# Moving V's base copy from VectorE to GpSimd through an fp32 staging tile, with one more VectorE exponential batch and a longer ride allowance

## The chip, the cores and the metric

One core of a Trainium2 chip is used; the jobs ran on two chips, 0 and 6, and every kernel is compared with the kernel before in its own job. The metric is device time in microseconds (us) of one execution; a kernel is run three to twelve times and the median is quoted. Engines: PE is TensorE (matmul), PEld its weight loads, DVE is VectorE, ACT is ScalarE, POOL is GpSimd.

## The reference

Multi-head attention for x of 2048 x 448, 16 heads of 28:

```python
qkv = (x @ wqkv).reshape(B, S, 3, H, Dh).transpose(2, 0, 3, 1, 4)
q, k, v = qkv[0], qkv[1], qkv[2]
scores = einsum("bhqd,bhkd->bhqk", q, k) * Dh ** -0.5
o = einsum("bhqk,bhkd->bhqd", softmax(scores), v)
out = o.transpose(0, 2, 1, 3).reshape(B, S, D) @ wo
```

## The kernel before

The work is cut into 16 units: one group of four heads times 512 queries. A unit has 16 key tiles times 4 heads = 64 score tiles of 128x512 in PSUM. Most of them go through ACT (exponential, to bf16 slots in `PT`), in groups of three and two tiles. The others, four key tiles of each unit, five in the units of `D_FIVE` and three in the last, are "batches" for DVE: an integer approximation of the exponential, made as a sum of four terms. A batch costs DVE four evictions (`PD` from PSUM, one for each head) and two int16 steps, and it costs PE four PV passes instead of one. All PV passes of a unit accumulate in one PSUM bank (`ACC`), which DVE copies out (`OTS`) when the unit is complete; I say that a unit closes then. Units are numbered from 0 to 15.

```python
D_FIVE = (3, 5, 7, 9, 11)
...
NPT = 36                                  # PT slots for exponentials
VX = sb("VX", [128, 3, 2 * GD], FP32)     # GD = 112
...
P.pool("M", [5, 6])                       # two PSUM banks for projections and DVE score tiles
```

V of a group and a chunk of 512 keys is projected into a bank of `M`; DVE reads that bank twice, once for the bf16 base copy `V` and once for the key tiles that batches need, as fp32 `VX`, from which POOL makes four scaled copies `VC`:

```python
def proj_v(g, c, prio):
    ... # 16 matmuls into one bank
    ev1, ev2 = job(f"pv_{g}_{c}", prio, mms,
                   (Vd <- bank[:, 0:4*GD]),                       # base copy, bf16
                   extra=(tensor_copy VX[:, xs, 0:nb*GD] <- some key tiles of bank))
    v_ev[(g, c)] = ev1
    for j in range(NTERM):                                         # NTERM = 4
        sc = P.add("pool", tensor_scalar VC <- VX * TERM_C[j], deps=[ev2, ...], dur=450)
```

(The lambdas are shortened here.) The order of instructions on each engine is not written by hand. The kernel has a list scheduler that simulates the engines with estimated durations when the kernel is built, and emits the order that it found. Part of it is the ride rule. Score matmuls of different heads use different rows of the PE array, so several issued together cost hardly more than one: in the trace of run C below, four issued together at 240.54 us took 0.40 us, a single one at 242.24 us 0.39 us. A score tile for DVE therefore waits for an ACT group with other heads to ride with, up to an allowance:

```python
RIDE = 8000.0     # ns
...
if op.ride:
    near = prev is not None and prev.kind == "r" and not self.burst & set(op.heads) and ...
    if not near:
        st = max(st, ready_t[i] + op.ride)
```

A last step puts filler matmuls of zeros into the gaps in PE's order that the scheduler foresees, to keep PE's activity up.

## Time and profile before

| kernel before | |
|---|---|
| median of the first three runs | 373.45 us (372.86 to 374.69) |
| busy PE, DVE, ACT | 93%, 92%, 93% of the span |
| busy POOL | 19% |

The profiled run is another one. It took 375.33 us (span 373.5 us), more than any of the timed runs, and its spans and idle times should be read with that in mind.

The page of the profile, cut to the lines that matter. Part 1 gives busy us, share of the span and the number of instructions by engine; part 4 the engines' shares of the chain of waits; part 5 the groups: line, engine, operation, output<-input, count | busy us, mean ns | idle us of the engine just before them and what ended it.

```profile
PE 346.7 (93%) x3953; PEld 108.7 (29%) x3953; DVE 342.2 (92%) x530; ACT 347.8 (93%) x306; POOL 70.9 (19%) x142
...
DVE 49%; PE 30%; ACT 14%; DMA 2%; issue 2%; SPq 0%
...
L898 ACT ACTIVATE PT<-ps 128x1024 bf16<-128x1024 f32 (+1 forms) x301 | 344.6, 1266 | 7.3 <-PE ps L857 5.5
L917 DVE TENSOR_SCALAR PD<-ps 128x512 int16<-128x512 f32 x272 | 177.4, 680 | 9.3 <-PE ps L857 7.6
L857 PE MATMUL ps<-QT,KT 28*128 28x512 bf16 x1024 | 149.0, 384 | 7.9 <-ACT PT L898 3.0
...
L925 DVE TENSOR_SCALAR PD<-PD 128x4096 int16<-128x4096 int16 x68 | 83.9, 1236 | 0.1
...
L712 POOL TENSOR_TENSOR QT<-RB,OTS 128x128 bf16<-128x128 f32 x60 | 36.1, 632 | 159.6 <-DMA RB<-scr_r 159.6
...
L923 DVE TENSOR_SCALAR PD<-PD 128x2048 int16<-128x2048 int16 x68 | 47.3, 703 | 0.1
...
L800 PE MATMUL ps<-ZM,ZW 128*32 128x512 bf16 x160 | 13.8, 383 | 0.0
```

Three engines are within one per cent of each other, and the chain of waits passes through all three. L857 are the score matmuls. L809 are the PV passes and L800 the fillers.

The groups of DVE with their shapes kept apart, the three lines of V's evictions:

```profile
L497 DVE CAST V<-ps 128x448 bf16<-128x448 f32 x16 | 9.8, 615 | 0.0
...
L551 DVE COPY VX<-ps 128x112 f32<-128x112 f32 x12 | 3.2, 264 | 0.0
L551 DVE COPY VX<-ps 128x224 f32<-128x224 f32 x4 | 1.5, 376 | 0.0
```

The second eviction is 4.7 us busy in all; by start times in the timeline it holds up the next instruction by 0.18 or 0.30 us each, 3.4 us in all.

Busy us of each engine in stretches (from:to, length, then PE, PEld, DVE, ACT, POOL, each with its count, then granted clock, DMA share, GB/s):

```profile
30.00:328.00 298.00, 283.60 (x3247) 86.35 (x3243) 294.03 (x447) 292.93 (x257) 54.58 (x101) 1.00 0.06 17
...
328.00:358.00 30.00, 27.99 (x307) 7.93 (x304) 27.15 (x43) 29.98 (x28) 4.39 (x8) 1.00 0.13 39
```

Up to 328 us DVE and ACT are both busy over 98% of the time; after that ACT alone is.

### The profile page before, as it was taken

The numbers are of one execution on the slowest core, as the hardware profiler recorded it, in microseconds if no ns is written. First come the engines' busy times: TensorE is split into PE (matmuls) and PEld (weight loads), VectorE is DVE, ScalarE is ACT, GpSimd is POOL, SyncE is SP. The second block draws the span as 40 slices with busy tenths as digits, with TensorE's granted clock in tenths as the row PEclk, the third lists the DMA queues.
The fourth block names the chain that finished last, engine by engine and source line by source line (L and its number), as shares of the span: only waits on it lengthen the run. The fifth ranks groups of instructions, "written<-read, shape, count | busy, mean of one in ns | idle before, by whom it ended". The sixth has DMA issues, their size and how long they took to land.

```text
span 373.5 us, 9127 instructions
## 1 busy us (share of the span) xinstructions
PE 346.7 (93%) x3953; PEld 108.7 (29%) x3953; DVE 342.2 (92%) x530; ACT 347.8 (93%) x306; POOL 70.9 (19%) x142
## 2 busy tenths in 40 slices
PE   7899999989999999998999999999998999999992
PEld 2342232323322323232223223332222223222231
DVE  1699999999999999999999999999999999999832
ACT  2799999999999999999999999999999999999971
POOL 7212021221401321041201303212030302002100
PEclk9899999999999999999999999999999999999998
DMA  9900010100001010010100000000000002110201
GB/s 172 194 21 2 12 37 2 32 2 18 16 3 32 3 31 2 4 31 2 32 2 14 21 5 29 2 10 24 21 12 4 31 15 67 38 29 18 80 0 58
DMA packets 21623, 10.49 MB, mean 28 GB/s; under 512 B 15757, under 2 KB 19597, under 8 KB 21577
## 3 DMA queue, kind: packets, MB, share of 16 engines
q1 hardware_dynamic: 20152, 9.54, 10.7%
q8 instruction: 32, 0.52, 0.6%
q10 hardware_dynamic: 1424, 0.31, 0.5%
q14 instruction: 15, 0.11, 0.1%
HBM read 5.66 MB, written 2.08 MB: 21 GB/s over the span
## 4 chain that ended last, share of the span: by engine, by line
DVE 49%; PE 30%; ACT 14%; DMA 2%; issue 2%; SPq 0%
DVE PD L917 24%; ACT PT L898 14%; PE ps L857 12%; DVE PD L925 11%; PE ps L809 10%; DVE PD L923 6%; PE ps L520 4%; DVE QT L495 2%; DVE OTS L695 2%; PE ps L542 2%; DMA xT<-in_x_dram 1%; DVE V L497 1%; DVE OUTS L679 1%; DVE KT L497 1%; PE ps L667 1%
## 5 line engine op out<-in xcount | busy, mean ns | idle before, releaser
L898 ACT ACTIVATE PT<-ps 128x1024 bf16<-128x1024 f32 (+1 forms) x301 | 344.6, 1266 | 7.3 <-PE ps L857 5.5
L917 DVE TENSOR_SCALAR PD<-ps 128x512 int16<-128x512 f32 x272 | 177.4, 680 | 9.3 <-PE ps L857 7.6
L857 PE MATMUL ps<-QT,KT 28*128 28x512 bf16 x1024 | 149.0, 384 | 7.9 <-ACT PT L898 3.0
L809 PE MATMUL ps<-PD,VC 128*32 128x512 bf16 x1088 | 91.3, 384 | 3.7 <-DVE PD L925 2.0
L925 DVE TENSOR_SCALAR PD<-PD 128x4096 int16<-128x4096 int16 x68 | 83.9, 1236 | 0.1
L857 PEld LDWEIGHTS ps<-QT,KT 28*128 28x128 bf16 x1024 | 38.2, 91 | 130.5 <-ACT PT L898 74.4
L809 PE MATMUL ps<-PT,V 128*32 128x512 bf16 x752 | 66.5, 384 | 3.5 <-DVE OTS L695 3.5
L712 POOL TENSOR_TENSOR QT<-RB,OTS 128x128 bf16<-128x128 f32 x60 | 36.1, 632 | 159.6 <-DMA RB<-scr_r 159.6
L558 POOL TENSOR_SCALAR VC<-VX 128x112 bf16<-128x112 f32 (+1 forms) x64 | 28.1, 438 | 121.9 <-DVE VX L551 118.9
L923 DVE TENSOR_SCALAR PD<-PD 128x2048 int16<-128x2048 int16 x68 | 47.3, 703 | 0.1
L520 PE MATMUL ps<-xT,w_raw 128*32 128x512 bf16 x512 | 39.8, 391 | 2.2 <-DVE PD L917 1.1
L809 PEld LDWEIGHTS ps<-PD,VC 128*32 128x32 bf16 x1088 | 22.7, 94 | 43.7 <-issue 15.9
L809 PEld LDWEIGHTS ps<-PT,V 128*32 128x32 bf16 x752 | 17.4, 94 | 32.3 <-issue 19.9
L542 PE MATMUL ps<-w_raw,xT 128*128 128x112 bf16 x256 | 19.1, 217 | 1.2 <-DVE PD L917 1.0
L542 PEld LDWEIGHTS ps<-w_raw,xT 128*128 128x128 bf16 x256 | 13.5, 99 | 11.5 <-issue 6.7
L520 PEld LDWEIGHTS ps<-xT,w_raw 128*32 128x32 bf16 x512 | 10.5, 95 | 21.5 <-issue 10.2
L800 PE MATMUL ps<-ZM,ZW 128*32 128x512 bf16 x160 | 13.8, 383 | 0.0
L667 PE MATMUL ps<-wop,QT 128*128 128x448 bf16 x48 | 13.2, 357 | 0.2 <-DVE PD L917 0.2
L497 DVE CAST KT<-ps 128x512 bf16<-128x512 f32 x16 | 11.0, 685 | 1.9 <-PE ps L520 1.8
L495 DVE TENSOR_SCALAR QT<-ps 128x512 bf16<-128x512 f32 x15 | 10.3, 686 | 0.2
L695 DVE COPY OTS<-ps 128x512 f32<-128x512 f32 x15 | 10.2, 679 | 0.1
L497 DVE CAST V<-ps 128x448 bf16<-128x448 f32 x16 | 9.8, 615 | 0.0
(49 smaller groups left out, 56.1 us busy)
## 6 DMA issues: line engine op xcount, KB each, us to landing
RB<-scr_r SPq DMA_DIRECT2D x60, 64.0 KB, 2.0
out_dram<-OUTS SPq DMA_DIRECT2D x16, 112.0 KB, 1.7
w_raw<-in_wqkv_dram SPq DMA_DIRECT2D x3, 249.0 KB, 4.1
wop<-in_wo_dram SPq DMA_DIRECT2D x16, 24.5 KB
w_raw<-in_wqkv_dram ACTq DMA_DIRECT2D x3, 87.0 KB, 4.2
scr_l<-OTS SPq DMA_DIRECT2D x15, 8.0 KB
LT<-scr_l SPq DMA_DIRECT2D x15, 8.0 KB, 1.7
scr_r<-RS SPq DMA_DIRECT2D x15, 8.0 KB, 1.4
```

The costliest lines, as they stand in the source:

```text
L495: fe = (lambda e: e.tensor_scalar(evac[0](), evac[1](hold[0].banks[0]), mul, None, ALU.mult))
L497: fe = (lambda e: e.tensor_copy(evac[0](), evac[1](hold[0].banks[0])))
L520: ins = e.matmul(ps[32 * h:32 * h + 32, b * 512:(b + 1) * 512], w_raw[:, it, col:col + 32], xT[:, it, c * 512:(c + 1) * 512], start=(it == ...
L542: ins = e.matmul(ps[:, b * 512 + j * GD:b * 512 + (j + 1) * GD], xT[:, it, n * 128:(n + 1) * 128], w_raw[:, it, 2 * D + g * GD:2 * D + (g ...
L558: sc = P.add("pool", (lambda e, dst=dst, j=j: e.tensor_scalar(dst, src, TERM_C[j], 1.0, ALU.mult, ALU.mult)), deps=[ev2, ms_c1[j]], after= ...
L712: nm = P.add("pool", (lambda e, k=k: e.tensor_tensor(QT[:, g, c * QCH + k * w_:c * QCH + (k + 1) * w_], RB[:, ub, k * w_:(k + 1) * w_], OT ...
L809: return e.matmul(ps[32 * h:32 * h + 32, ACC * 512:(ACC + 1) * 512], lhsT, rhs, start=first, stop=False, skip_group_check=True, tile_posit ...
L857: return e.matmul(bank(b), KT[32 * h:32 * h + DH, g, kt * 128:(kt + 1) * 128], QT[32 * h:32 * h + DH, g, c * QCH:(c + 1) * QCH], start=Tru ...
L898: ex = P.add("act", (lambda e, p0=p0, w=w, b0=b0: e.activation(PT[:, p0 * 512:(p0 + w) * 512], bank(b0, w), AF.Exp, scale=ESCALE)), deps=[ ...
L917: r = P.add("dve", (lambda e, hold=hold, zs=zs, h=h: e.tensor_scalar(PD[:, zs, 0, h * 512:(h + 1) * 512], bank(hold[0].banks[0]), ZBIAS, 0 ...
L923: h1 = P.add("dve", (lambda e, zs=zs: e.tensor_scalar(PD[:, zs, 1, :], PD[:, zs, 0, :], float(TERM_D[1]), None, ALU.add)), deps=rs_ + [z_l ...
L925: h2 = P.add("dve", (lambda e, zs=zs: e.tensor_scalar(PD[:, zs, 2:4, :], PD[:, zs, 0:2, :], float(TERM_D[2]), None, ALU.add)), deps=[h1] + ...
```

## The change

Its intent: let DVE read each V bank once, into an fp32 staging tile that holds all four key tiles; let POOL, which is idle most of the time, make the bf16 base copy from there; spend the DVE time that this frees on one more batch (in unit 13), which takes four score tiles off ACT. The ride allowance goes from 8 to 10 us.

```diff
-D_FIVE = (3, 5, 7, 9, 11)
+D_FIVE = (3, 5, 7, 9, 11, 13)
...
-        VX = sb("VX", [128, 3, 2 * GD], FP32)
+        VX = sb("VX", [128, 3, 4 * GD], FP32)
... (job() loses its second eviction)
-            ev1, ev2 = job(f"pv_{g}_{c}", prio, mms, ((lambda: Vd), ...), evac_dur=545,
-                           extra=((lambda e, b: e.tensor_copy(VX[:, xs, 0:nb * GD]..., bank(b)...[:, j0:4:js, :])), ...))
-            v_ev[(g, c)] = ev1
+            ev = job(f"pv_{g}_{c}", prio, mms,
+                     ((lambda: VX[:, xs, :]), (lambda b: bank(b)[:, 0:4 * GD]), vx_last[xs]), evac_dur=545)
+            v_ev[(g, c)] = []
+            for k in range(2):
+                Vd = V[:, 4 * c + 2 * k:4 * c + 2 * k + 2, ...]
+                vs = VX[:, xs, 2 * k * GD:(2 * k + 2) * GD]...
+                sc = P.add("pool", (lambda e, Vd=Vd, vs=vs: e.tensor_scalar(Vd, vs, 1.0, 1.0, ALU.mult, ALU.mult)),
+                           deps=[ev, ms_v1], after=[sc], dur=520, ...)
+                v_ev[(g, c)].append(sc)
... (the scaled copies now read VX with a step, and wait for ev)
-        RIDE = 8000.0
+        RIDE = 10000.0
```

More of the change, by code (lines that the diff above doesn't have):

```diff
@@ L479, in _fast, with job @@
         job_last = []
-        def job(name, prio, mm_ops, evac, evac_eng="dve", evac_dur=610, mul=None, extra=None):
+        def job(name, prio, mm_ops, evac, evac_eng="dve", evac_dur=610, mul=None):
             hold = []
@@ L497, in job @@
                 fe = (lambda e: e.tensor_copy(evac[0](), evac[1](hold[0].banks[0])))
-            if extra is None:
-                ev = P.add(evac_eng, fe, deps=[prev] + list(evac[2:]), dur=evac_dur, prio=-100.0, name=f"{name}_ev", rel=[(hold[0], 0)])
-                if prio > 0.5:
-                    job_last.append(ev)
-                return ev
-            ev1 = P.add(evac_eng, fe, deps=[prev] + list(evac[2:]), dur=evac_dur, prio=-100.0, name=f"{name}_ev")
-            ev2 = P.add("dve", (lambda e: extra[0](e, hold[0].banks[0])), deps=[prev] + list(extra[2:]), after=[ev1], dur=extra[1], prio=-100.0,
-                        name=f"{name}_ev2", rel=[(hold[0], 0)])
+            ev = P.add(evac_eng, fe, deps=[prev] + list(evac[2:]), dur=evac_dur, prio=-100.0, name=f"{name}_ev", rel=[(hold[0], 0)])
             if prio > 0.5:
-                job_last.append(ev2)
-            return ev1, ev2
+                job_last.append(ev)
+            return ev
         kq_ev = {}
@@ L547, in proj_v @@
             vx_n[0] += 1
-            Vd = V[:, 4 * c:4 * c + 4, g * 128:(g + 1) * 128].rearrange("p n (h r) -> p n h r", r=32)[:, :, :, 0:DH]
-            ev1, ev2 = job(f"pv_{g}_{c}", prio, mms,
-                           ((lambda: Vd), (lambda b: bank(b)[:, 0:4 * GD].rearrange("p (n h d) -> p n h d", n=4, d=DH)), ms_v1), evac_dur=545,
-                           extra=((lambda e, b: e.tensor_copy(VX[:, xs, 0:nb * GD].rearrange("p (n d) -> p n d", n=nb),
-                                                           bank(b)[:, 0:4 * GD].rearrange("p (n d) -> p n d", d=GD)[:, j0:4:js, :])), 130 + 90 * nb, vx_last[xs]))
-            v_ev[(g, c)] = ev1
-            src = VX[:, xs, 0:nb * GD].rearrange("p (n h d) -> p n h d", n=nb, d=DH)
-            sc = None
+            ev = job(f"pv_{g}_{c}", prio, mms,
+                     ((lambda: VX[:, xs, :]), (lambda b: bank(b)[:, 0:4 * GD]), vx_last[xs]), evac_dur=545)
+            sc = None
+            v_ev[(g, c)] = []
+            for k in range(2):
+                Vd = V[:, 4 * c + 2 * k:4 * c + 2 * k + 2, g * 128:(g + 1) * 128].rearrange("p n (h r) -> p n h r", r=32)[:, :, :, 0:DH]
+                vs = VX[:, xs, 2 * k * GD:(2 * k + 2) * GD].rearrange("p (n h d) -> p n h d", n=2, d=DH)
+                sc = P.add("pool", (lambda e, Vd=Vd, vs=vs: e.tensor_scalar(Vd, vs, 1.0, 1.0, ALU.mult, ALU.mult)),
+                           deps=[ev, ms_v1], after=[sc], dur=520, prio=g * 4 + c - 2.0, name=f"vb{g}_{c}_{k}")
+                v_ev[(g, c)].append(sc)
+            src = VX[:, xs, :].rearrange("p (n h d) -> p n h d", n=4, d=DH)[:, j0:4:js, :, :]
             for j in range(NTERM):
@@ L558, in proj_v @@
                 sc = P.add("pool", (lambda e, dst=dst, j=j: e.tensor_scalar(dst, src, TERM_C[j], 1.0, ALU.mult, ALU.mult)),
-                           deps=[ev2, ms_c1[j]], after=[sc], dur=450, prio=g * 4 + c, name=f"vc{g}_{c}_{j}")
+                           deps=[ev, ms_c1[j]], after=[sc], dur=450, prio=g * 4 + c, name=f"vc{g}_{c}_{j}")
             vc_ev[(g, c)] = sc
@@ L822, in pv_a @@
             op = pv_common(u, kt, f"PV{u}_{kt}", f_pv, list({id(tile_ev[(u, kt, h)]): tile_ev[(u, kt, h)] for h in range(4)}.values())
-                           + [v_ev[(g, kt // 4)]], u + (kt + 4) / NK)
+                           + v_ev[(g, kt // 4)], u + (kt + 4) / NK)
             for s in slots:
```

## The prediction

> **What bounds it now.** The page's busy line has PE 93%, DVE 92%, ACT 93%: three engines in balance. By stretches (the windows view), from 30 to 328 us DVE is busy 294.0 of 298 us and ACT 292.9; from 328 to 358 us ACT 29.98 of 30 and DVE 27.2. The chain of waits changes between DVE, PE and ACT until 331 us, then is one run of 24 exponentials to 358 us, then a serial end of 10 us. So DVE and ACT bind together to about 328 us, ACT alone after that.
>
> **Removed.** The second V eviction: 12 copies of 128x112 (264 ns) and 4 of 128x224 (376 ns). In the timeline they move the next start by only 0.18 and 0.30 us, so DVE wins 12*0.18+4*0.30 = 3.4 us. The first eviction now writes fp32 staging instead of bf16 V; I expect it to stay near 615 ns (the 128x512 evictions take 679 ns to fp32, 685 to bf16). Its PSUM bank comes free about 0.2 us sooner.
>
> **Added.** One VectorE batch: start to start 4*0.60+0.60+1.13 = 4.13 us of DVE, and three more PV passes on PE (0.22 us each, 0.65 us). ACT loses four of 752 tiles at 344.6/752 = 0.458 us: 1.83 us. GpSimd gets 32 casts of 128x224, about 0.43 us each as the scaled copies of that shape (1.71 us for four undisturbed), 14 us in all; it is busy only 71 us. It has to cast from SBUF, having no access to PSUM (Trainium skill, "GPSIMD Engine Reference", Specifications). Casts could queue behind the normalising multiplies that wait for a DMA, but V jobs run most of a unit ahead. At the start V of chunk 0 should be ready near 14.2 us; the first PV starts at 16.7.
>
> **Contention.** The Trainium skill ("SBUF — State Buffer", Who interferes with whom) says that a VectorE operation in a two-port mode and a GpSimd operation exclude each other. The trace agrees: scaled copies take 286 to 1422 ns, and the int16 DVE steps (medians 683, 1217 ns) reach 996 and 1527 when they meet GpSimd. I take today's DVE loss as about 3 us over 124 GpSimd operations, so 0.8 us more from 32 more (an estimate from these spreads).
>
> **On the path.** DVE: -3.4+4.1+0.8 = +1.5 us, but the new batch lies in unit 13, near 300-325 us, and the last two units have slack for most of it. ACT, which binds the end, gets 1.8 us shorter. PE +0.65 us, partly replacing filler matmuls. The larger ride allowance (8 to 10 us): about neutral. If ACT's own idle (7.3 us) doesn't grow, the kernel is 1.8 us shorter; I expect 0.3 us to be given back. The static order is computed anew; I allow 2 us either way for that.
>
> Predicted: 371.9 us, range 369.4 to 375.2; faster by over 2%: 3%, within 2%: 94%, slower: 3%.
>
> **What would show it.** Groups: exponentials near 342.8 us busy; PD evictions x276, int16 steps x69, their means up by 0-20 ns; staging copy 128x448 x16 near 615 ns; 32 POOL casts at 0.43-0.6 us. Busy line: DVE 342-345, POOL 86-90. No notable PE wait on POOL. Last exponential ending near 357 us.
>
> **What would make it wrong.** DVE the sole limit, so that +1.5 us shows in full and ACT's gain turns into idle (375); GpSimd locking out the int16 steps far oftener; V casts stuck behind a multiply that waits for its DMA; a slower fp32 eviction; or a reshuffled order that holds the two PSUM banks longer.

## The result, and the profile after

| | before | after |
|---|---|---|
| median of six runs, us | 373.5 (372.86 to 374.69) | 371.95 (371.26 to 372.73) |
| ratio | | 0.9954, 95% interval 0.9931 to 0.9977 |

A ratio is the mean time of one kernel's runs over that of the other's of the same rounds, so it is not quite the ratio of the medians quoted. Executions over 1.5% slower than the fastest of the same kernel are left out of the means. The change is within 2%, and it is a gain that the interval separates from zero.

The page after:

```profile
PE 342.3 (92%) x4033; PEld 110.3 (30%) x4033; DVE 342.8 (92%) x520; ACT 345.4 (93%) x304; POOL 83.7 (23%) x174
...
DVE 52%; PE 37%; ACT 5%; DMA 3%; issue 2%; SPq 0%; DVEq 0%
...
L894 ACT ACTIVATE PT<-ps 128x1536 bf16<-128x1536 f32 (+1 forms) x299 | 342.2, 1273 | 6.8 <-PE ps L853 5.1
L913 DVE TENSOR_SCALAR PD<-ps 128x512 int16<-128x512 f32 x276 | 180.4, 680 | 8.1 <-PE ps L853 7.0
L853 PE MATMUL ps<-QT,KT 28*128 28x512 bf16 x1024 | 140.1, 385 | 8.7 <-ACT PT L894 5.3
...
L921 DVE TENSOR_SCALAR PD<-PD 128x4096 int16<-128x4096 int16 x69 | 84.5, 1226 | 0.1
...
L919 DVE TENSOR_SCALAR PD<-PD 128x2048 int16<-128x2048 int16 x69 | 47.8, 698 | 0.1
...
L548 POOL TENSOR_SCALAR V<-VX 128x224 bf16<-128x224 f32 x32 | 15.7, 508 | 103.1 <-DVE VX L497 103.0
...
L796 PE MATMUL ps<-ZM,ZW 128*32 128x512 bf16 x228 | 18.9, 382 | 0.0
```

V's only eviction in the groups of DVE by shape, and the stretches:

```profile
L497 DVE COPY VX<-ps 128x448 f32<-128x448 f32 x16 | 9.8, 613 | 0.3 <-PE ps L535 0.2
```

```profile
30.00:328.00 298.00, 279.70 (x3349) 87.33 (x3345) 292.80 (x438) 293.84 (x257) 64.12 (x126) 1.00 0.06 17
328.00:358.00 30.00, 28.93 (x294) 8.79 (x294) 29.27 (x45) 29.62 (x26) 4.91 (x8) 1.00 0.15 43
```

What I had forecast of the parts is there: the eviction costs the same to fp32 (613 ns) as to bf16 (615 ns); DVE is busy 342.8 us (forecast 342 to 345) and ACT's exponentials 342.2 us (342.8); the 32 casts take 508 ns on average. The list of waits has one wait of a PE weight load on a cast, of 0.2 us. In the start, V of chunk 0 is cast from 13.3 to 14.0 us and the first PV begins at 16.6 us.

Two numbers were in no term of my sum. The score matmuls are busy 140.1 us instead of 149.0, although their count is the same; and the fillers grew from 160 to 228. The same number of score matmuls in less time means that they overlap more; run C below, where only the ride allowance differs, ties that to the allowance. Because of the fillers PE's busy time as a whole fell by only 4.4 us.

An identity is useful here: the span is the start of the first exponential, plus the busy time of the exponentials, plus ACT's idle time between them, plus what follows the last one. Before: 10.0+344.6+6.8+12.1 = 373.5 us. After: 9.8+342.2+6.4+12.4 = 370.8 us. (The 0.5 us in front of the first exponential is taken from the idle time; the last exponential ends at 361.4 and 358.4 us.) By this sum of two profiles, the gain is ACT's busy time, much as predicted. But these two spans differ by 2.7 us, where the medians differ by 1.6 us, since the profiled run of the kernel before was a long one. And such a sum is bookkeeping: it says where time was saved, not which part of the change saved it. That took experiments.

### The profile page after: what moved, and what is told of

Read it like the earlier page. It is cut to its first block, busy times and chain, and to the rows that moved or that the text cites. A ratio compares the mean times of both kernels' runs of the same rounds, so it can differ in the third digit from the quotient of the medians.

```text
span 370.8 us, 9316 instructions
## 1 busy us (share of the span) xinstructions
PE 342.3 (92%) x4033; PEld 110.3 (30%) x4033; DVE 342.8 (92%) x520; ACT 345.4 (93%) x304; POOL 83.7 (23%) x174
## 4 chain that ended last, share of the span: by engine, by line
DVE 52%; PE 37%; ACT 5%; DMA 3%; issue 2%; SPq 0%; DVEq 0%
DVE PD L913 26%; PE ps L805 14%; DVE PD L921 13%; PE ps L853 13%; DVE PD L919 7%; ACT PT L894 4%; PE ps L513 4%; PE ps L663 2%; PE ps L535 2%; DVE KT L497 2%; DVE OTS L691 1%; DMA xT<-in_x_dram 1%; DVE QT L495 1%; DVE VX L497 1%; DMA LT<-scr_l 1%
## 5 line engine op out<-in xcount | busy, mean ns | idle before, releaser
L894 ACT ACTIVATE PT<-ps 128x1536 bf16<-128x1536 f32 (+1 forms) x299 | 342.2, 1273 | 6.8 <-PE ps L853 5.1
L913 DVE TENSOR_SCALAR PD<-ps 128x512 int16<-128x512 f32 x276 | 180.4, 680 | 8.1 <-PE ps L853 7.0
L853 PE MATMUL ps<-QT,KT 28*128 28x512 bf16 x1024 | 140.1, 385 | 8.7 <-ACT PT L894 5.3
L921 DVE TENSOR_SCALAR PD<-PD 128x4096 int16<-128x4096 int16 x69 | 84.5, 1226 | 0.1
L708 POOL TENSOR_TENSOR QT<-RB,OTS 128x128 bf16<-128x128 f32 x60 | 32.8, 577 | 167.8 <-DMA RB<-scr_r 167.8
L805 PE MATMUL ps<-PT,V 128*32 128x512 bf16 x748 | 65.1, 384 | 2.1 <-DVE OTS L691 1.9
L513 PE MATMUL ps<-xT,w_raw 128*32 128x512 bf16 x512 | 38.7, 391 | 1.5 <-DVE PD L913 0.9
L548 POOL TENSOR_SCALAR V<-VX 128x224 bf16<-128x224 f32 x32 | 15.7, 508 | 103.1 <-DVE VX L497 103.0
L554 POOL TENSOR_SCALAR VC<-VX 128x112 bf16<-128x112 f32 (+1 forms) x64 | 29.0, 453 | 3.0
L796 PE MATMUL ps<-ZM,ZW 128*32 128x512 bf16 x228 | 18.9, 382 | 0.0
L663 PE MATMUL ps<-wop,QT 128*128 128x448 bf16 x48 | 14.2, 358 | 1.2 <-DVE PD L913 0.9
L497 DVE CAST KT<-ps 128x512 bf16<-128x512 f32 x16 | 10.9, 682 | 1.8 <-PE ps L513 1.8
```

Of the source, the lines that this page charges most:

```text
L497: fe = (lambda e: e.tensor_copy(evac[0](), evac[1](hold[0].banks[0])))
L513: ins = e.matmul(ps[32 * h:32 * h + 32, b * 512:(b + 1) * 512], w_raw[:, it, col:col + 32], xT[:, it, c * 512:(c + 1) * 512], start=(it == ...
L554: sc = P.add("pool", (lambda e, dst=dst, j=j: e.tensor_scalar(dst, src, TERM_C[j], 1.0, ALU.mult, ALU.mult)), deps=[ev, ms_c1[j]], after=[ ...
L663: return e.matmul(bank(hold[0].banks[0])[:, 0:D], QT[:, gg, n * 128:(n + 1) * 128], wop[:, gg, :], start=(gg == 0), stop=(gg == G - 1))
L708: nm = P.add("pool", (lambda e, k=k: e.tensor_tensor(QT[:, g, c * QCH + k * w_:c * QCH + (k + 1) * w_], RB[:, ub, k * w_:(k + 1) * w_], OT ...
L805: return e.matmul(ps[32 * h:32 * h + 32, ACC * 512:(ACC + 1) * 512], lhsT, rhs, start=first, stop=False, skip_group_check=True, tile_posit ...
```

## The experiments

Theory P is the prediction's: DVE and ACT limit together, ACT's 1.8 us are the gain, the staging pays the batch's DVE time, and the ride allowance is neutral. Rivals: D, DVE alone limits; S, the recomputed order decides whatever the busy times are; and, after the first results, R, PE is a limit as well, which the ride allowance relieves.

Call the staging A, the batch B, the ride allowance C. The six kernels with some of the three were run, each against the kernel before.

### A: the staging alone

```diff
 (the whole change, but)
+D_FIVE = (3, 5, 7, 9, 11)
+RIDE = 8000.0
```

> The staging alone, without the batch and with the old ride allowance: DVE loses 3.4 us of copies and gains perhaps 0.8 us of lock-outs, ACT's work stays as before. Theory P (ACT and DVE limit together, ACT binds the end): at most 0.5 us shorter, ratio 0.998 to 1.000, and DVE idle grows by about 2.5 us. Rival D (DVE is the sole limit): 2.6 us shorter, ratio 0.993. Rival S (the recomputed order decides): anything from 0.993 to 1.006, unrelated to the busy times.

Measured: 376.93 us, ratio 1.0106 (1.0074 to 1.0138). No theory but a wide form of S held: slower, although DVE's busy time fell from 342.2 to 339.5 us. Two things make up part of it. The time exceeds the recorded span by 3.6 us here (median), by about 1.8 us in the kernel before; the median span is 373.45 us against 371.8 us of the kernel before in the same job. And three of the six runs had a mean granted clock of 0.980 to 0.986, with spans of 373.9 to 375.5 us; the three at 0.994 and above had 372.2 to 373.0 us, where the kernel before at such clocks had 371.3 to 372.5. In the profile DVE's idle time in front of the evictions is 10.9 us, against 9.3 before: most of it waiting for score matmuls.

### B: the batch alone

```diff
 (the kernel before, but)
+D_FIVE = (3, 5, 7, 9, 11, 13)
```

> The sixth five-batch unit alone, no staging, old ride allowance: DVE +4.1 us, ACT -1.8 us, PE +0.65 us. Theory P: the new batch lies late and the last two units absorb part of it, so between 1 us shorter and 1.5 us longer, ratio 0.997 to 1.004. Rival D: 4.1 us longer, ratio 1.011. Rival S: within 0.993 to 1.006. The order up to unit 12 should be nearly that of before.

Measured: 377.85 us, ratio 1.0102 (1.0075 to 1.0128); one of its six runs was slow and isn't in the ratio (median without it 377.42 us). That is the number that D gives, but B+C below has the same DVE work and the ratio 0.9986, so the work alone doesn't explain it. The profile shows where: the accumulator of unit 14 is evicted at 351.3 us instead of 340.8, and 14.4 us follow the last exponential instead of 12.1. My claim that "the last two units have slack for most of it" fails in this order. It doesn't fail for want of the staging alone: B+C closes unit 14 at 341.2 us.

### C: the ride allowance alone

```diff
 (the kernel before, but)
+RIDE = 10000.0
```

> The ride allowance 10 us instead of 8 alone; no instruction is added or removed. Theories P and D: ratio 0.998 to 1.002. Rival S: the order changes in many places, so up to 2 us either way (0.995 to 1.005); this run measures how much a mere reordering is worth.

Measured: 374.74 us, ratio 1.0028 (1.0013 to 1.0044): slightly slower. The profile is more telling than the time. Score matmuls fall from 149.0 to 139.7 us and by 236 us ACT has done 195 exponentials since 12 us, against 192 (about one of the three is owed to the start, where the profile of before had a stall of 1.65 us and this one 0.47; B, with the allowance of 8 us, had 194). No work is added, but the fillers are placed anew: 240 instead of 160.

```profile
L857 PE MATMUL ps<-QT,KT 28*128 28x512 bf16 x1024 | 139.7, 384 | 10.3 <-ACT PT L898 5.4
L800 PE MATMUL ps<-ZM,ZW 128*32 128x512 bf16 x240 | 20.3, 383 | 0.0
```

Then it loses that in one stall. ACT's timeline of the kernel before around 240 us, then that of C (start, length, and in brackets the idle time before and what ended it):

```profile
236.27 6.88 ACT L898 ACTIVATE PT<-ps 128x1024 bf16<-128x1024 f32 x6 [0.24 <-PE ps L857]
243.99 21.50 ACT L898 ACTIVATE PT<-ps 128x1024 bf16<-128x1024 f32 x19 [0.83 <-PE ps L809]
```

```profile
235.86 4.62 ACT L898 ACTIVATE PT<-ps 128x1024 bf16<-128x1024 f32 x4 [0.23 <-PE ps L857]
244.11 73.95 ACT L898 ACTIVATE PT<-ps 128x1024 bf16<-128x1024 f32 x65 [3.62 <-PE ps L809]
```

In C the accumulator of unit 9 is evicted only at 242.9 us, in the middle of a stretch where DVE is never idle (the eviction in the timeline, then the stretch):

```profile
242.92 0.68 DVE L695 COPY OTS<-ps 128x512 f32<-128x512 f32 x1
...
240.00:250.00 10.00, 8.64 (x103) 2.23 (x95) 10.00 (x15) 6.38 (x7) 1.74 (x3) 1.00 0.03 4
```

Until then unit 10's PV passes cannot start, so no slot of `PT` comes free, and ACT stops. That is my reading of the timeline; the experiment with more slots below tests it.

### A and B without C

```diff
 (the whole change, but)
+RIDE = 8000.0
```

> The whole change but for the ride allowance, which stays 8 us. Theory P: as the whole change, ratio 0.995 to 0.997 against the kernel before. If the ride allowance is a needed part of the change (it lets the five-batch unit 13 run), the gain is lost here: 0.999 or more. Rival S: 0.993 to 1.004.

Measured: 375.43 us, ratio 1.0063 (1.0034 to 1.0093). So the ride allowance, "about neutral" in my prediction, is a needed part: the whole change has 0.9954, a difference of 1.1%, about 4 us. Not all of that is the order: the runs with a mean clock of 0.994 or more have spans of 371.9 to 373.0 us here and of 369.5 to 370.9 us with the whole change, some 2 to 3 us apart; three runs here, at 0.986 to 0.991, had 374.3 to 376.5 us. Score matmuls and fillers:

```profile
L853 PE MATMUL ps<-QT,KT 28*128 28x512 bf16 x1024 | 145.5, 384 | 8.7 <-ACT PT L894 4.3
L796 PE MATMUL ps<-ZM,ZW 128*32 128x512 bf16 x144 | 12.3, 383 | 0.0
```

Against these the whole change has 5.4 us less of score matmuls and 6.6 us more of fillers, so PE's busy time as a whole is the same (341.9 and 342.3 us). No run tells what the fillers cost or bring.

### A and C without the batch

```diff
 (the whole change, but)
+D_FIVE = (3, 5, 7, 9, 11)
```

> Staging and the 10 us ride allowance, without the sixth five-batch unit: DVE about 1.5 us less work than before, ACT as before. Theory P (the gain of the whole change is ACT's 1.8 us): 1.5 to 1.8 us longer than the whole change, so ratio 0.999 to 1.001 against the kernel before, and the last exponential ends about 1.8 us later than with the whole change. Rival S (the recomputed order decides; single parts gave 1.003 to 1.011): anything from 0.994 to 1.012. Rival D (DVE limits): faster than the whole change, below 0.995.

Measured: 372.33 us, ratio 0.9955 (0.9937 to 0.9972). This is the result that contradicts theory P most: without the batch, and so with all of ACT's old work, the kernel has the ratio of the whole change (0.9954). With the staging unit 9 closes at 238.0 us instead of 242.9, and the stall is gone:

```profile
238.01 0.68 DVE L691 COPY OTS<-ps 128x512 f32<-128x512 f32 x1
...
ACT PT L894 <- PE ps L853: 4.2, 16, 0.5
...
ACT PT L894 <- PE ps L805: 0.4, 1, 0.4
```

(The eviction, and ACT's waits in this kernel: us in total, times, longest.) Against C alone the staging is worth 0.73%, 2.7 us.

### B and C without the staging

```diff
 (the kernel before, but)
+D_FIVE = (3, 5, 7, 9, 11, 13)
+RIDE = 10000.0
```

> The batch and the 10 us ride allowance, without the staging: DVE +4.1 us, ACT -1.8 us. The batch alone had 1.010, with a serial end 2.3 us longer behind the last exponential because unit 14 closed 10 us later. Theory P amended (the staging pays the batch's VectorE time): again slower than before, 1.003 to 1.010, with unit 14 closing late. Rival S: the ride allowance alone repairs it, 0.996 to 1.001.

Measured: 372.58 us, ratio 0.9986 (0.9963 to 1.0009). The rival's forecast; unit 14 closes at 341.2 us, not late. It has the same stall as C, 3.6 us. Yet the profiled run, with that stall in it, has a span of 370.0 us, no longer than the 370.8 us of the whole change, which has no such stall. So what the stall costs is not shown.

The eight kernels together; score matmul busy time and ACT's idle time before exponentials are from one profile each.

| kernel | ratio | lowest to highest us | score matmuls, us | ACT idle, us |
|---|---|---|---|---|
| before | 1 | 373.04 to 375.07 | 149.0 | 7.3 |
| A | 1.0106 | 375.77 to 379.78 | 142.9 | 7.0 |
| B (fast runs) | 1.0102 | 375.81 to 378.34 | 150.5 | 8.1 |
| A+B | 1.0063 | 373.70 to 378.26 | 145.5 | 7.3 |
| C | 1.0028 | 374.19 to 375.08 | 139.7 | 7.9 |
| A+C | 0.9955 | 371.17 to 372.43 | 137.5 | 5.2 |
| B+C | 0.9986 | 371.79 to 374.32 | 138.4 | 7.6 |
| A+B+C, the change | 0.9954 | 371.26 to 372.73 | 140.1 | 6.8 |

Each part alone is slower (1.06%, 1.02% and 0.28%), and all three together are 0.46% faster. The sum of single effects is useless here. Added alone to C, staging and batch each gain (0.73% and 0.42%); added alone to the kernel before, each loses. But added to a kernel that has the other already, each gains at 8 us too (A+B is 0.4% below A and below B), and at 10 us the batch gains nothing (A+C and the whole change). The score matmuls have a mean of 147.0 us in the four kernels with 8 us and of 138.9 us in the four with 10 us.

### The order kept, one cost put back at a time

The eight kernels above differ in the order of thousands of instructions, so a difference of one per cent between two of them can be the order's. The next four keep the whole change's order on every engine: the scheduler sees the same durations, and only an extra instruction is emitted beside its twin. All gave correct results. The whole change had been timed in an earlier job; the kernel before had a median of 373.5 to 373.6 us in every job, so I compare ratios.

DVE: the second copies back.

```diff
+    def fe(e):
+        fe0(e)                                   # the staging copy
+        return again(e, hold[0].banks[0])        # the old second copy, into a scratch tile
```

> The whole change in its own instruction order, with only the 16 old second copies issued again after the staging copy (into a scratch tile; result correct): DVE +3.4 us, nothing reordered. Against the whole change: theory P (DVE has slack in part) +0.5 to +1.5 us, so ratio 0.997 to 1.000 to the kernel before; theory D (DVE binds wherever it is full) +3.0 to +3.6 us, ratio 1.003 to 1.005; rival S (the order decided): under +0.5 us, ratio 0.995 to 0.997.

Measured: 373.28 us, ratio 1.0005 (0.9979 to 1.0032). The added copies have their old durations (261 and 376 ns); DVE's busy time rose by 2.3 us, to 345.1. Against 0.9954 this is 0.5%, 1.9 us (1.3 us by the medians) for the 3.4 us by which such copies hold up DVE: between P and D, and the intervals allow 0.6 to 3.2 us (an estimate). So a us of DVE time is worth about half a us, between 0.2 and 0.9, where these copies lie, from 13 to 242 us; the last three units were not tested.

The run shows one thing more. With the old copies back, unit 9 still closes at 238.5 us, and ACT has no long wait:

```profile
238.51 0.68 DVE L701 COPY OTS<-ps 128x512 f32<-128x512 f32 x1
...
ACT PT L904 <- PE ps L863: 4.0, 14, 0.5
```

So it is the order found with the staging, and not the DVE time that the staging frees, that keeps the stall of C away.

ACT: 1.9 us back in unit 13.

```diff
+    if twice is not None:                        # two exponentials of 128x1024 in unit 13
+        e.activation(PX[:, :], bank(b0, w), AF.Exp, scale=ESCALE)
     return e.activation(PT[...], bank(b0, w), AF.Exp, scale=ESCALE)
```

> The whole change in its own order, with two exponentials of 128x1024 in unit 13 issued twice (the first into a scratch tile; result correct): ACT +1.9 us there, which is what the batch took off. Theory P (ACT binds the end): +1.5 to +1.9 us against the whole change, ratio 0.999 to 1.001 to the kernel before; theory D: +0 to +0.5 us, ratio 0.995 to 0.997.

Measured: 375.04 us, ratio 1.0032 (1.0005 to 1.0059): 0.8% more than the whole change, 2.9 us, which is more than was added. The profile has an accident in it. Stretches of this kernel:

```profile
296.00:300.00 4.00, 2.16 (x27) 0.66 (x23) 2.72 (x5) 4.00 (x5) 0.03 (x1) 0.83 0.00 0
300.00:302.00 2.00, 2.00 (x19) 0.33 (x11) 1.45 (x2) 1.31 (x2) 0.00 (x0) 0.50 0.04 8
302.00:304.00 2.00, 1.63 (x16) 0.43 (x14) 1.61 (x3) 1.79 (x3) 0.00 (x0) 0.98 0.00 0
```

While ACT repeats its exponentials PE has little to do (busy 2.16 of 4 us), the granted clock drops to 0.50, and PE, now slow, delays ACT in turn (ACT waits 0.69 us for scores at 301.4 us, right after 16 fillers that took 1.90 us). The whole change has a clock of 1.00 in all three stretches. The Trainium skill ("TensorE: Matmul & The Clock Gate", Part 1) describes it so: the clock is half unless recent activity releases it. The trace agrees, with 0.50. The three runs with a mean clock of 0.991 or more had spans of 371.7, 372.7 and 372.1 us, 1.6 to 2.6 us over the whole change's median span of 370.15 us. So ACT time in unit 13 is on the path in full or nearly so, as P says (the intervals allow 1.6 to 4.2 us for the 2.0 us by which ACT's busy time grew, an estimate), and can cost the clock on top.

PE: score matmuls back.

```diff
+    if twice:                                    # one head of every second batch, 35 in all
+        s_one(e, hold[0].banks[0], u, kt, h)
     return s_one(e, hold[0].banks[0], u, kt, h)
```

> The whole change in its own order, with one score matmul of every second batch (35 in all) issued twice into the same bank (result correct): PE +35*0.216 = +7.5 us of score work, which is about what the 10 us ride allowance saved (score matmuls busy 145.5 us with 8 us, 140.1 with 10 us). If PE limits too (theory R: the ride allowance gains because it frees PE): +2 to +5 us against the whole change, ratio 1.001 to 1.009 to the kernel before. If PE has slack (my prediction counted it as unimportant): under +1 us, ratio below 0.998.

Measured: 375.41 us, ratio 1.0058 (1.0037 to 1.0078). The group of score matmuls:

```profile
L853 PE MATMUL ps<-QT,KT 28*128 28x512 bf16 x1059 | 147.7, 384 | 6.8 <-ACT PT L894 3.3 <-DVE PD L917 1.5 <-ACT QT L493 0.7
```

That is 7.6 us more than in the whole change, and it costs 1.04%, 3.9 us. Theory R holds: PE is a limit too, and a us of score matmuls costs about half a us (0.36 to 0.66 by the intervals, an estimate). It is not the clock: four of the six runs had 0.997 or more and spans of 373.3 to 373.8 us. The extra matmuls stand just in front of DVE's evictions, so this is the price there and not of any PE time.

POOL: each cast twice.

```diff
+    e.tensor_scalar(V2[:, y, :]..., vs, 1.0, 1.0, ALU.mult, ALU.mult)     # scratch
     return e.tensor_scalar(Vd, vs, 1.0, 1.0, ALU.mult, ALU.mult)
```

> The whole change in its own order, with each of the 32 V casts on GpSimd issued twice (the first into a scratch tile; result correct): POOL +14 to +17 us. My prediction put the lock-outs of 32 casts at 0.8 us of VectorE time, half of it on the path: +0.2 to +0.8 us against the whole change, ratio 0.996 to 0.998, means of the two int16 steps up by 3 to 15 ns. If the exclusion costs far more: +2 us or more. If nothing: within 0.3 us.

Measured: 371.87 us, ratio 0.9952 (0.9934 to 0.9970): nothing. POOL's busy time rose to 98.3 us and DVE's by 0.7 us to 343.5, where I had put 0.8 us for 32 casts; the two int16 steps:

```profile
L925 DVE TENSOR_SCALAR PD<-PD 128x4096 int16<-128x4096 int16 x69 | 85.1, 1235 | 0.1
L923 DVE TENSOR_SCALAR PD<-PD 128x2048 int16<-128x2048 int16 x69 | 48.2, 702 | 0.1
```

They are 9 and 4 ns longer than in the whole change. That is hardly above the scatter: f3 and f4, which keep the same order and add no cast, have DVE at 343.3 and 343.2 us. Nor is it a full test: the second cast of a pair follows the first at once and never took longer than 380 ns, so only the first of each pair met VectorE. The mutual exclusion that the Trainium skill ("SBUF — State Buffer", Who interferes with whom) describes shows mostly on the other side: the casts of 371 ns undisturbed go up to 1287 ns in the profile of the whole change, and POOL has the time.

### Two tests of the slots

B+C with 40 slots for exponentials instead of 36; because a group of three never wraps, 35 of the 36 and all 40 are usable.

```diff
 (B+C, but)
-    NPT = 36
+    NPT = 40
```

> Batch and 10 us ride allowance without staging (that kernel gave 0.9986, with one 3.6 us stall of the exponentials at 240 us behind the late accumulator eviction of unit 9), now with 40 instead of 36 slots for exponentials. If the stall is ACT running out of its 35 usable slots while VectorE is late (theory Q), five more slots let ACT run 2.3 us further ahead: the stall falls to about 1.3 us and the kernel gets 1.5 to 3 us shorter, ratio 0.991 to 0.995, below the whole change. If the stall is not about slots, it stays at 3.6 us and the ratio stays 0.997 to 1.001.

Measured: 376.98 us, ratio 1.0091 (1.0065 to 1.0118). The stall did what theory Q said: from 3.6 us to 1.4 us, with 1.3 forecast. ACT's waits in B+C, then with 40 slots:

```profile
ACT PT L898 <- PE ps L809: 3.6, 1, 3.6
```

```profile
ACT PT L898 <- PE ps L809: 1.4, 1, 1.4
```

The time did the opposite of the forecast. The order was recomputed as well; in the profile (span 376.2 us) unit 14 closes at 352.1 us, 15.9 us follow the last exponential, and the clock drops in unit 13:

```profile
310.00:315.00 5.00, 5.00 (x49) 1.12 (x47) 3.15 (x5) 3.19 (x3) 0.00 (x0) 0.60 0.26 77
```

So the stall was about slots, and removing most of it did not make a faster kernel.

The whole change with 38 slots (`NPT = 38`), a candidate and a control.

> The whole change with 38 instead of 36 slots for exponentials (three more usable ones), a candidate for a faster kernel and a control: the whole change has no stall over 0.7 us behind the slots after the start, so theory Q expects little, 0 to 1 us shorter, ratio 0.993 to 0.996; the recomputed order differs in few places.

Measured: 373.54 us, ratio 0.9985 (0.9945 to 1.0025), from 370.89 to 376.09. The two runs with clocks of 0.998 and 1.000 had spans of 369.6 and 369.1 us, the two at 0.995 had 371.0 and 372.4, the two at 0.986 and 0.990 had 374.2 and 373.4. The profiled one lost its clock in the last unit, where DVE and ACT then wait for PE:

```profile
350.00:355.00 5.00, 5.00 (x23) 1.02 (x22) 2.47 (x5) 3.58 (x4) 0.00 (x0) 0.50 0.13 36
```

One kernel, one order, and 5 us between runs, by and large longer where the mean clock is lower; that all of it is the clock's doing in the last units is not shown, since only one of these runs was profiled. No version tried beats the whole change; A+C equals it.

## Why the prediction was right or wrong

The time was right: 371.9 us forecast, 371.95 us measured. The account behind it was right in its costs and half wrong in its causes.

- **Costs of the parts: right.** Eviction 613 ns, casts 508 ns, DVE 342.8 us, exponentials 342.2 us, PE hardly ever waiting for a cast. The exclusion between DVE and POOL: 0.8 us of DVE time forecast; doubling the casts gave 0.7 us, which is hardly above the scatter, and no time lost. Smaller misses: POOL is busy 83.7 us, not 86 to 90, and the means of the int16 steps fell (1236 to 1226 and 703 to 698 ns) instead of rising by up to 20.
- **"ACT, which binds the end, gets 1.8 us shorter": right for ACT, wrong as the source of the gain.** ACT time in unit 13 is on the path (f3). But the batch's net worth is nil, within about 1.1 us (an estimate from the intervals): A+C has 0.9955 without it, the change 0.9954 with it. The prices that the kept-order runs suggest give about that, -0.6 us as an estimate: 1.8 us of ACT gained, against about half of 4.1 us of DVE and half of 0.65 us of PE. If that holds, I was wrong to let the last two units absorb most of the DVE time; but the DVE price was measured before 242 us, not there.
- **The staging only pays for the batch: wrong.** With the 10 us allowance it gains 2.7 us alone (A+C against C). The 1.9 us that f1 puts on the freed DVE time would be most of it. The stall of 3.6 us is gone as well, but f1 shows that the new order removes it, not the freed time, and B+C, which has the stall, had a profiled span no longer than the whole change's.
- **"The larger ride allowance: about neutral": wrong; this is the step that failed.** It takes 5 to 12 us off the score matmuls (5.4 us between A+B and the whole change), and the whole change without it has 1.0063. I had listed PE at 93% and then costed only the batch's 0.65 us on it. f4 shows a price of about half a us for each us of score matmuls, so 5.4 us would be worth about 2.8 us (an estimate), which is what A+B and the whole change differ by at like clocks; the rest of their 4 us went with lower clocks. Alone, the allowance puts ACT about two exponentials ahead by 236 us, and the stall takes them back. Why the parts don't add up is not shown: each kernel has its own order.
- **"I allow 2 us either way" for the new order: too little.** Single parts gave +4 us, and one kernel varied by 5 us between runs. That the total fell within 0.1 us is partly luck: terms mis-sized in opposite directions cancelled (the allowance brings more than nothing, the batch less than 1.8 us).
- **A misread line:** I let the exponentials end at 358 us because the chain of waits left ACT there. They ran on to 361.4 us; the chain had moved to the PV passes that ended later.

Open: why A alone is slower at 8 us. Its further 1.8 us outside the recorded span, its lower clock in three runs and more waiting of DVE for score tiles make up what was measured, but none was tested by itself. The same holds for how much of the time of B and of the 40-slot kernel is due to the clock. Also open is what the fillers do, whose number changes with the allowance: no run leaves them out.

## What to carry to other kernels

When three engines are within one per cent of each other, price each of them by putting one cost back in a kept order before adding up savings: here a us of ACT in a late unit cost about a full us, DVE and the score matmuls on PE about half, and 15 us more of POOL nothing that could be measured. A parameter that adds no work, like the ride allowance, can be the largest term; look at busy times whose counts did not change. And test the parts of a combined change alone and in pairs: here every part alone was a loss.

## What the Trainium skill lacked or had wrong

- "TensorE: Matmul & The Clock Gate" gives half clock after PE has been idle, which agrees with 0.50 here. It tells of the ramp at the start, of clocks lost behind DMA waits and of clocks that swing behind short idles between groups of matmuls. It lacks what one sees here: a drop in the last unit of a kernel that keeps PE busy 92% of the span, and mean clocks that differ from run to run of that kernel, which went with 5 us of difference (spans 369.1 us at a mean clock of 1.000, 374.2 us at 0.986).
- "SBUF — State Buffer" describes the exclusion between VectorE and GpSimd as a full block for the second to issue. It lacks what that amounts to in a kernel: here, with 32 more GpSimd casts, VectorE's busy time was 0.7 us higher, hardly above the scatter, and the kernel lost no time.
- "Runtime: NRT & Kernel Launch" has a gap between the profile's total time and the reported execution time, the same for every kernel. It lacks, and I found no page that has, that a kernel's time can exceed the span from its first to its last instruction by a different amount in each kernel: about 1.8 us in most, 2.2 us with the casts doubled, 3.3 to 4.3 us in the six runs with the staging alone.
